# Block-sparse attention with a gated MLP on one core: gMLP products of batch 0 dealt one a slot, and the last spatial product in two halves with a transposition moved to ScalarE

## The chip, the cores and the metric

The kernel runs on one core of a Trainium2 chip. The metric is the device time of one execution in microseconds (us); lower is better. Short names: PE is TensorE, PEld its weight loads, DVE is VectorE, ACT is ScalarE, POOL is GpSimd, SP is SyncE. SP and ACT can also issue DMAs; SPq and ACTq are their DMA issues in the profile.

## The reference

Attention with a block mask over 4 batches, 8 heads, 768 positions and 64 dimensions a head, and a gated MLP with a spatial product (gMLP) on its output:

```
scores = q @ k.T / sqrt(64), masked outside band, edge and sampled blocks
x      = softmax(scores) @ v, heads side by side          # (4, 768, 512)
h      = relu(x @ w_in);  u, v = two halves of h          # 512 columns each
v_n    = (v - mean) / sqrt(var + 1e-6)                    # over the columns
v_s    = w_spatial @ v_n + b_spatial                      # over the 768 positions
out    = (u * v_s) @ w_out                                # float32
```

## The kernel before, in words

The 768 positions are six chunks of 128 (`tcc` 0 to 5 in the code). Work is in bfloat16 with float32 sums in PSUM.

**Slots.** The order of all instructions is written out by hand (`manual_schedule`). The main loop (L882) runs over slots. From slot 36 on, a slot does one sixth of one head: `qk_full` issues two score matmuls (L487) into a PSUM tile `ps` and one exponential on ACT (L491) that reads it; `av_full` issues six matmuls with the values (L538) for the head seven slots behind. The tile `ps` has the tag `sc`, of which there are two buffers: the score matmuls of slot s can start only when the exponential of slot s-2 has read its tile. Behind these, `run_queue(STEPS.get(s))` (L896) takes a number of gMLP matmul steps from a queue. For slots 20 to 97 that number stands in the dictionary `STEPS` (L816); from slot 98 on it is dealt evenly.

**The gMLP of a batch** (class `Moe`) is a list of products. Each is made by `product` (L610): some matmuls of 512 columns into one PSUM tile (all at L617), the last followed by `done`, which takes the result out. `v_product` and `u_product` make v and u. `s_product` is the spatial product of one chunk: six matmuls, and then one DVE instruction (L689) that adds the bias and multiplies by u, in place in the tile `un`. Behind every second chunk it issues a DMA transposition from `un` into `gt` (L699) on SP. `o_product` is the product with `w_out`: four matmuls that read `gt` as weights, an eviction to `osb` by ACT or DVE, and the DMA of the output (L718).

**The last batch** (`self.last`) has its spatial and output products behind the loop (L901), where PE has nothing else to do. There the transposition of chunks 0 and 1 and that of chunks 2 and 3 are each one DMA, and chunks 4 and 5 have one each: G01, G23, G4 and G5 below. The spatial products are called s0 to s5 and the output products o0 to o5; o5 is already in two halves of 256 columns, o5a and o5b. ACT evicts o0, o2, o4 and o5b, DVE o1, o3 and o5a. ACT issues the output DMAs of o0, o1, o2 and o5b, SP those of o3, o4 and o5a. Every engine runs its instructions in their order, and an instruction that waits holds up all behind it. PSUM tiles of the tail go round three tags (`tail_tags`, L594), six banks in all.

Of the kernel before, what the change touches and what calls it, by code (L numbers as in the profile page):

```python
# [14 lines left out]
ALU = mybir.AluOpType  # L15
# [11 lines left out]
def kernel(  # L27
# [16 lines left out]
    nc = tc.nc  # L44
# [5 lines left out]
    NCH = S // 128  # L50
# [3 lines left out]
    DH = DFF // 2  # L54
# [24 lines left out]
    w_spt = const.tile([128, NCH, NCH, 128], BF16)  # L79
    b_col = const.tile([128, NCH], FP32)  # L80
# [517 lines left out]
    def moe_ps(last):  # L598
        if not (last or ended):
            return psum.tile([128, 512], FP32, tag=moe_tag(), bufs=1, name="ps_moe")  # L600
        if not last:
            return psum.tile([128, 1024], FP32, tag="sc", bufs=2, name="ps_sc")[:, 0:512]
        tail_tags.rotate(1)
        if tail_tags[0] == "sc":
            return psum.tile([128, 1024], FP32, tag="sc", bufs=2, name="ps_sc")[:, 0:512]
        if tail_tags[0] == "moe":
            return psum.tile([128, 512], FP32, tag=moe_tag(), bufs=1, name="ps_t")
        return psum.tile([128, 512], FP32, tag="av", bufs=2, name="ps_t")

    def product(n, lhs, rhs, last, done, w=512):  # L610
        ref = {}
        out = []
        for i in range(n):
            def run(i=i):
                if i == 0:
                    ref["ps"] = moe_ps(last)
                nc.tensor.matmul(out=ref["ps"][:, 0:w], lhsT=lhs(i), rhs=rhs(i),  # L617
                                 start=(i == 0), stop=(i == n - 1))
                if i == n - 1:
                    done(ref["ps"][:, 0:w])  # L620
            out.append(run)
        return out
# [6 lines left out]
    class Moe:  # L629
# [55 lines left out]
                           self.last, done)  # L685

        def s_product(self, tcc):
            def done(ps):
                nc.vector.scalar_tensor_tensor(out=self.un[:, tcc, :], in0=ps,  # L689
                                               scalar=b_col[:, tcc:tcc + 1],  # L690
                                               in1=self.un[:, tcc, :], op0=ALU.add,
                                               op1=ALU.mult)
                if self.last and tcc >= NCH - 2:
                    g0 = tcc
                elif tcc % 2 == 1:
                    g0 = tcc - 1
                else:
                    return
                nc.sync.dma_start_transpose(  # L699
                    out=self.gt[:, g0:tcc + 1].rearrange("p t c n -> p (t c) n"),  # L700
                    in_=self.un[:, g0:tcc + 1, :].rearrange("p t d -> p (t d)"))
            return product(NCH, lambda s: w_spt[:, tcc, s, :], lambda s: self.vn[:, s, :],
                           self.last, done)

        def o_product(self, tcc):
            steps = []
# [37 lines left out]
    def deal(steps, slots):  # L744
        queue.extend(steps)
        pace["slots"], pace["credit"] = slots, 0.0

    def run_queue(n=None):
        if n is not None:
            for _ in range(n):  # L750
                queue.popleft()()
            return
        if not queue or pace["slots"] <= 0:
            return
        pace["credit"] += (len(queue) - pace["credit"]) / pace["slots"]
        pace["slots"] -= 1
        n = int(pace["credit"] + 0.5)
        for _ in range(min(n, len(queue))):
            queue.popleft()()
            pace["credit"] -= 1  # L760
# [5 lines left out]
    def when(slot, *fns):  # L766
        at.setdefault(slot, []).extend(fns)
# [45 lines left out]
    when(18, lambda: first["steps"].popleft()())  # L813
    when(20, close_first)
    when(29, lambda: deal(moe[0].in_steps("v2 v3 u2 u3", TC), 14))
    STEPS = {20: 0, 21: 3, 22: 2, 23: 0, 24: 2, 25: 1, 26: 2, 27: 2, 28: 0, 29: 1, 30: 1, 31: 1, 32: 2, 33: 1, 34: 1, 35: 1, 36: 1, 37: 0, 38: 1, 39: 2, 40: 2, 41: 2, 42: 1, 43: 3, 44: 3, 45: 0, 46: 2, 47: 1, 48: 2, 49: 1, 50: 2, 51: 0, 52: 2, 53: 1, 54: 1, 55: 1, 56: 1, 57: 2, 58: 1, 59: 1, 60: 1, 61: 2, 62: 2, 63: 1, 64: 1, 65: 1, 66: 1, 67: 2, 68: 2, 69: 1, 70: 1, 71: 1, 72: 1, 73: 1, 74: 2, 75: 1, 76: 1, 77: 2, 78: 1, 79: 1, 80: 1, 81: 1, 82: 0, 83: 2, 84: 1, 85: 2, 86: 0, 87: 1, 88: 1, 89: 2, 90: 2, 91: 0, 92: 2, 93: 2, 94: 2, 95: 2, 96: 2, 97: 2}  # L816
    when(42, lambda: deal(moe[0].in_steps("v4 v5 u4 u5", TC) + moe[0].rest_steps(),
                          S0 + 8 + 48 - 42))
    for b in (1, 2):
# [62 lines left out]
    for s in range(NS + LAG + 2):  # L882
# [11 lines left out]
        for f in early:  # L894
            f()
        run_queue(STEPS.get(s))  # L896
        for f in late.get(s, []):
# [34 lines left out]
```

## Time and profile before

| what | us |
|---|---|
| median of 3 runs | 209.09 (209.01 to 209.22) |
| the profiled execution, its own time | 209.45 |
| its span, first to last instruction | 207.6 |
| PE busy | 202.7 |
| ACT busy | 167.0 |
| DVE busy | 129.9 |

The profile is of one execution. Times in it run from the start of the span. The granted clock of PE is 1.00 in it. A line of a timeline gives start, length, engine, line of the code, operation, tiles and number of instructions; instructions of one kind that follow each other are merged, and a bracket at the end is idle time of the engine before it and what ended that. A DMA landing is the time from issue until its semaphore is complete.

### The profile page before, as it was taken

To read this page: it belongs to the slowest core of one execution; us is meant where nothing else is said; L and a number is where in the kernel's file an instruction comes from. 1 tells how busy PE (TensorE), PEld (TensorE's weight loads), DVE (VectorE), ACT (ScalarE), POOL (GpSimd) and SP (SyncE) were. 2 spreads that over 40 slices of the span, in tenths; PEclk is the share of its full clock that TensorE was granted. 3 is DMA by queue.
4 is the path that set the end of the run, shared out by engine and by line. 5 is a ranking of instruction groups with operands and counts; after the bars stand their busy time and mean duration, and the time that the engine had idled before them with its cause. 6 is when DMAs were issued, how large, how long until landed. Compare 5 with 4: busy or idle time off the path is not lost.

```text
span 207.6 us, 5255 instructions
## 1 busy us (share of the span) xinstructions
PE 202.7 (98%) x2128; PEld 127.2 (61%) x2128; DVE 129.9 (63%) x287; ACT 167.0 (80%) x222; POOL 75.4 (36%) x117
## 2 busy tenths in 40 slices
PE   8899999999999999999999999999999999999993
PEld 6689878766666666655655555655665556444441
DVE  7688697889654364648798355348685444567542
ACT  5899999999999999889999887998989883266022
POOL 6799899684680421310716402200202000003000
PEclk9999999999999999999999999999999999999999
DMA  5999999999999999999986549785101072810466
GB/s 141 345 364 347 345 406 297 234 278 303 230 356 193 264 272 171 319 318 262 299 91 182 162 88 279 179 246 125 38 3 38 0 92 51 285 72 0 50 152 255
DMA packets 65579, 42.21 MB, mean 203 GB/s; under 512 B 46740, under 2 KB 60436, under 8 KB 65556
## 3 DMA queue, kind: packets, MB, share of 16 engines
q1 hardware_dynamic: 64692, 40.78, 76.8%
q10 hardware_dynamic: 864, 1.11, 1.5%
q8 instruction: 16, 0.26, 0.5%
q14 instruction: 7, 0.06, 0.1%
HBM read 24.38 MB, written 6.29 MB: 148 GB/s over the span
## 4 chain that ended last, share of the span: by engine, by line
PE 93%; ACT 5%; issue 0%; DVE 0%; ACTq 0%
PE ps_moe L617 32%; PE ps L487 23%; PE ps_av L538 13%; PE ps_t L617 8%; PE ps L474 6%; PE ps_sc L617 5%; ACT a_all L479 5%; PE ps_av L520 4%; PE wps L182 1%; PE ps L302 1%; PE ps_av L302 1%; PE mq L309 0%; ACT osb L224 0%; PE psq L317 0%; PE ps L317 0%
## 5 line engine op out<-in xcount | busy, mean ns | idle before, releaser
L491 ACT ACTIVATE a_all<-ps 128x768 bf16<-128x768 f32 x144 | 112.8, 812 | 11.8 <-PE ps L487 5.3
L487 PE MATMUL ps<-kq 88*128 88x384 bf16 x288 | 70.4, 325 | 0.0
L538 PEld LDWEIGHTS <-a_all 128*128 128x128 bf16 x864 | 45.2, 97 | 20.0
L538 PE MATMUL ps_av<-vv,a_all 128*128 128x65 bf16 x864 | 49.8, 193 | 0.0
L487 PEld LDWEIGHTS <-kq 88*128 88x128 bf16 x288 | 27.7, 97 | 29.2 <-issue 0.3
L617 PE MATMUL ps_moe<-w_in_t,xt 128*128 128x512 bf16 x144 | 43.2, 378 | 0.0
L479 ACT ACTIVATE a_all<-ps 128x1024 bf16<-128x1024 f32 x36 | 34.1, 1026 | 2.5 <-PE ps L474 2.0
L617 PE MATMUL ps_moe<-vn,w_spt 128*128 128x512 bf16 x108 | 33.5, 378 | 0.0
L656 POOL TENSOR_SCALAR std<-mv 128x3 f32<-128x3 f32 (+1 forms) x9 | 2.9, 317 | 72.5 <-DVE mv L653 56.9
L138 POOL CAST nat<-st_k 128x768 bf16<-128x768 f32 (+2 forms) x18 | 14.6, 810 | 30.8 <-DMA st_k<-in_k_dram 29.9
L502 DVE RECIPROCAL rc<-ps_av 128x6 f32<-128x6 f32 (+1 forms) x36 | 6.7, 186 | 26.0 <-PE ps_av L538 23.2
L689 DVE SCALAR_TENSOR_TENSOR un<-ps_moe,b_col,un 128x512 bf16<-128x512 f32 x18 | 13.5, 749 | 14.8 <-PE ps_moe L617 14.8
L474 PE MATMUL ps<-kq 88*128 88x256 bf16 (+3 forms) x140 | 22.0, 279 | 0.7 <-ACT a_all L479 0.3
L617 PEld LDWEIGHTS <-xt 128*128 128x128 bf16 x192 | 15.4, 98 | 7.5 <-DVE xt L221 0.2
L503 DVE TENSOR_TENSOR xn<-ps_av,rc 128x384 bf16<-128x384 f32 (+1 forms) x36 | 18.5, 513 | 1.2
L617 PE MATMUL ps_moe<-w_out_t,gt 128*128 128x512 bf16 x60 | 17.6, 378 | 0.0
L652 DVE BATCH_NORM_STATS2 stats<-vn 128x6 f32<-128x512 bf16 x24 | 16.4, 683 | 1.3 <-ACT vn L647 0.9
L474 PEld LDWEIGHTS <-kq 88*128 88x128 bf16 (+1 forms) x140 | 12.8, 98 | 5.2 <-DVE kq L221 0.8
L138 POOL CAST nat<-st_q 128x768 bf16<-128x768 f32 (+2 forms) x21 | 14.8, 706 | 2.7 <-DMA st_q<-in_q_dram 2.2
L188 DVE TENSOR_SCALAR vn<-ps_moe 128x512 bf16<-128x512 f32 x18 | 12.3, 686 | 4.6 <-PE ps_moe L617 4.5
L617 PEld LDWEIGHTS <-w_spt 128*128 128x128 bf16 x144 | 11.7, 98 | 5.2
L221 DVE COPY kq<-tt 64x1536 bf16<-64x1536 bf16 x24 | 14.4, 598 | 0.4
(85 smaller groups left out, 208.7 us busy)
## 6 DMA issues: line engine op xcount, KB each, us to landing
st_v<-in_v_dram SPq DMA_DIRECT2D x16, 384.0 KB, 5.8
st_k<-in_k_dram SPq DMA_DIRECT2D x15, 384.0 KB, 4.7
out_dram<-osb SPq DMA_DIRECT2D x20, 256.0 KB, 2.8
st_q<-in_q_dram SPq DMA_DIRECT2D x12, 384.0 KB, 4.5
w_f<-in_moe_w_in_dram SPq DMA_DIRECT2D x6, 256.0 KB, 6.6
ws_f<-in_moe_w_spatial_dram SPq DMA_DIRECT2D x4, 384.0 KB, 7.2
w_f<-in_moe_w_out_dram SPq DMA_DIRECT2D x4, 256.0 KB, 4.2
st_q<-in_q_dram SPq DMA_DIRECT2D x6, 128.0 KB, 5.6
```

What stands on the lines that cost most here:

```text
L138: eng.tensor_copy(out=dst, in_=src)
L188: nc.vector.tensor_scalar(out=out, in0=in0, scalar1=s1, scalar2=s2, op0=o0, **kw)
L221: nc.vector.tensor_copy(out=o, in_=i)
L474: nc.tensor.matmul(out=ps[:, at:at + n * TW], lhsT=kq[0:kr, h, ci * 128:(ci + 1) * 128], rhs=kq[0:kr, h, qcols(t0, n)], start=True, stop=True)
L479: nc.scalar.activation(out=out, in_=ps, func=AF.Exp, scale=0.125)
L487: nc.tensor.matmul(out=ps[:, hf * 512:hf * 512 + HALF], lhsT=kq[0:KR, j % H, ci * 128:(ci + 1) * 128], rhs=kq[0:KR, j % H, S + hf * HALF:S ...
L491: nc.scalar.activation(out=a_ref["h", j][:, ci, :].rearrange("p (b c) -> p b c", b=2), in_=ps.rearrange("p (b c) -> p b c", b=2)[:, :, 0:H ...
L503: nc.vector.tensor_tensor(out=out, in0=ps[:, :, 0:D], in1=rc[:, 0:n].to_broadcast([128, n, D]), op=ALU.mult)
L538: nc.tensor.matmul(out=av_ref[j][:, qc, 0:VA], lhsT=a_ref["h", j][:, ci, qc * 128:(qc + 1) * 128], rhs=vv[p % NVV][:, h, ci, 0:VA], start= ...
L617: nc.tensor.matmul(out=ref["ps"][:, 0:w], lhsT=lhs(i), rhs=rhs(i), start=(i == 0), stop=(i == n - 1))
L652: nc.vector.bn_stats(out=stats, in_=self.vn[:, tcc, :])
L689: nc.vector.scalar_tensor_tensor(out=self.un[:, tcc, :], in0=ps, scalar=b_col[:, tcc:tcc + 1], in1=self.un[:, tcc, :], op0=ALU.add, op1=AL ...
```

## The change

The entries of `STEPS` for slots 82 to 91 go from 0, 2, 1, 2, 0, 1, 1, 2, 2, 0 to 1, 1, 1, 1, 1, 1, 1, 2, 1, 1; both sum to 11. In the last batch, the spatial product of chunk 5 is made as two products of 256 columns, each with its own PSUM tile, its own six matmuls and its own DVE instruction; G5 comes behind the second. G4 is issued by ACT; G01, G23 and G5 stay on SP.

```diff
         def s_product(self, tcc):
-            def done(ps):
...
+            parts = 2 if self.last and tcc == NCH - 1 else 1
+            w = DH // parts
+            steps = []
+            for i in range(parts):
+                cs = slice(i * w, (i + 1) * w)
+
+                def done(ps, i=i, cs=cs):
+                    nc.vector.scalar_tensor_tensor(out=self.un[:, tcc, cs], in0=ps,
+                                                   scalar=b_col[:, tcc:tcc + 1],
+                                                   in1=self.un[:, tcc, cs], op0=ALU.add,
+                                                   op1=ALU.mult)
+                    if i < parts - 1:
+                        return
...
-                nc.sync.dma_start_transpose(
+                    (nc.scalar if self.last and tcc == NCH - 2 else nc.sync).dma_start_transpose(
                         out=self.gt[:, g0:tcc + 1].rearrange("p t c n -> p (t c) n"),
                         in_=self.un[:, g0:tcc + 1, :].rearrange("p t d -> p (t d)"))
-            return product(NCH, lambda s: w_spt[:, tcc, s, :], lambda s: self.vn[:, s, :],
-                           self.last, done)
+                steps += product(NCH, lambda s: w_spt[:, tcc, s, :],
+                                 lambda s, cs=cs: self.vn[:, s, cs], self.last, done, w)
+            return steps
...
     STEPS = {
...
-        82: 0, 83: 2, 84: 1, 85: 2, 86: 0, 87: 1, 88: 1, 89: 2, 90: 2, 91: 0,
+        82: 1, 83: 1, 84: 1, 85: 1, 86: 1, 87: 1, 88: 1, 89: 2, 90: 1, 91: 1,
...
```

More of the change, by code (lines that the diff above doesn't have):

```diff
@@ L687, in s_product @@
         def s_product(self, tcc):
-            def done(ps):
[L689 to L701, printed above, removed]
-            return product(NCH, lambda s: w_spt[:, tcc, s, :], lambda s: self.vn[:, s, :],
-                           self.last, done)
+            parts = 2 if self.last and tcc == NCH - 1 else 1
[10 more added lines that the diff above has]
+                        return
+                    if self.last and tcc >= NCH - 2:
+                        g0 = tcc
+                    elif tcc % 2 == 1:
+                        g0 = tcc - 1
+                    else:
+                        return
+                    (nc.scalar if self.last and tcc == NCH - 2 else nc.sync).dma_start_transpose(
+                        out=self.gt[:, g0:tcc + 1].rearrange("p t c n -> p (t c) n"),
+                        in_=self.un[:, g0:tcc + 1, :].rearrange("p t d -> p (t d)"))
+                steps += product(NCH, lambda s: w_spt[:, tcc, s, :],
+                                 lambda s, cs=cs: self.vn[:, s, cs], self.last, done, w)
+            return steps
         def o_product(self, tcc):
@@ L815 @@
     when(29, lambda: deal(moe[0].in_steps("v2 v3 u2 u3", TC), 14))
-    STEPS = {20: 0, 21: 3, 22: 2, 23: 0, 24: 2, 25: 1, 26: 2, 27: 2, 28: 0, 29: 1, 30: 1, 31: 1, 32: 2, 33: 1, 34: 1, 35: 1, 36: 1, 37: 0, 38: 1, 39: 2, 40: 2, 41: 2, 42: 1, 43: 3, 44: 3, 45: 0, 46: 2, 47: 1, 48: 2, 49: 1, 50: 2, 51: 0, 52: 2, 53: 1, 54: 1, 55: 1, 56: 1, 57: 2, 58: 1, 59: 1, 60: 1, 61: 2, 62: 2, 63: 1, 64: 1, 65: 1, 66: 1, 67: 2, 68: 2, 69: 1, 70: 1, 71: 1, 72: 1, 73: 1, 74: 2, 75: 1, 76: 1, 77: 2, 78: 1, 79: 1, 80: 1, 81: 1, 82: 0, 83: 2, 84: 1, 85: 2, 86: 0, 87: 1, 88: 1, 89: 2, 90: 2, 91: 0, 92: 2, 93: 2, 94: 2, 95: 2, 96: 2, 97: 2}
+    STEPS = {20: 0, 21: 3, 22: 2, 23: 0, 24: 2, 25: 1, 26: 2, 27: 2, 28: 0, 29: 1, 30: 1, 31: 1, 32: 2, 33: 1, 34: 1, 35: 1, 36: 1, 37: 0, 38: 1, 39: 2, 40: 2, 41: 2, 42: 1, 43: 3, 44: 3, 45: 0, 46: 2, 47: 1, 48: 2, 49: 1, 50: 2, 51: 0, 52: 2, 53: 1, 54: 1, 55: 1, 56: 1, 57: 2, 58: 1, 59: 1, 60: 1, 61: 2, 62: 2, 63: 1, 64: 1, 65: 1, 66: 1, 67: 2, 68: 2, 69: 1, 70: 1, 71: 1, 72: 1, 73: 1, 74: 2, 75: 1, 76: 1, 77: 2, 78: 1, 79: 1, 80: 1, 81: 1, 82: 1, 83: 1, 84: 1, 85: 1, 86: 1, 87: 1, 88: 1, 89: 2, 90: 1, 91: 1, 92: 2, 93: 2, 94: 2, 95: 2, 96: 2, 97: 2}
     when(42, lambda: deal(moe[0].in_steps("v4 v5 u4 u5", TC) + moe[0].rest_steps(),
```

## The prediction

> **What bounds the kernel now.** I read the page's busy times and the chain that ended last first.
>
> ```profile
> PE 202.7 (98%) x2128; PEld 127.2 (61%) x2128; DVE 129.9 (63%) x287; ACT 167.0 (80%) x222; POOL 75.4 (36%) x117
> PE 93%; ACT 5%; issue 0%; DVE 0%; ACTq 0%
> ```
>
> PE is busy nearly throughout and the chain runs along it. So a microsecond that PE stands still is a microsecond of the total, and one saved comes out at the end as long as nothing else ends later there. "Busy" hides short stalls, because the ends of matmuls are modelled; stalls are read from starts. Next, therefore, PE's timeline around slot 82 (the score matmuls at 77.08 are the 47th pair), with ACT's for the same stretch and the stretch as one row.
>
> ```profile
> 77.08 0.49 PE L487 MATMUL ps<-kq 88*128 88x384 bf16 x2
> 77.41 0.35 PE L538 MATMUL ps_av<-vv,a_all 128*128 128x65 bf16 x6
> 77.75 0.48 PE L487 MATMUL ps<-kq 88*128 88x384 bf16 x2
> ...
> 78.68 0.49 PE L487 MATMUL ps<-kq 88*128 88x384 bf16 x2
> ...
> 79.41 0.49 PE L487 MATMUL ps<-kq 88*128 88x384 bf16 x2
> ...
> 80.35 0.49 PE L487 MATMUL ps<-kq 88*128 88x384 bf16 x2
> ...
> 80.86 0.49 PE L487 MATMUL ps<-kq 88*128 88x384 bf16 x2
> ...
> 81.74 0.48 PE L487 MATMUL ps<-kq 88*128 88x384 bf16 x2
> ```
>
> ```profile
> 76.16 2.96 ACT L491 ACTIVATE a_all<-ps 128x768 bf16<-128x768 f32 x4
> ```
>
> ```profile
> L491 ACT ACTIVATE a_all<-ps 128x768 bf16<-128x768 f32 x144 | 112.8, 812 | 11.8 <-PE ps L487 5.3
> ```
>
> ```profile
> 77.08:84.86 7.78, 7.78 (x93) 4.90 (x91) 4.50 (x10) 7.28 (x10) 1.66 (x2) 1.00 1.26 238
> ```
>
> Start to start, slot 84 with one gMLP step takes 79.41 - 78.68 = 0.73, slot 85 with two takes 0.94, slot 86 with none 0.51. But slot 82, also with none, takes 77.75 - 77.08 = 0.67, and slot 87 with one takes 0.88. Both are about 0.15 too long. Four exponentials take 2.96, each 0.81 long (the page's group, 812 ns), so one starts every (2.96 - 0.81)/3 = 0.72. The second of them, slot 81's, ends near 76.16 + 0.72 + 0.81 = 77.69, and slot 83's scores start at 77.75: they wait for its PSUM tile. A slot without a gMLP step is shorter than an exponential, so two slots later PE waits for ACT.
>
> Then the tail, in the timeline of SP and PE's weight loads, with each transposition's time to landing.
>
> ```profile
> 198.66 1.22 SPq L699 DMA_TRANSPOSE gt<-un  x1
> ```
>
> ```profile
> 199.98 1.22 SPq L699 DMA_TRANSPOSE gt<-un  x1
> ```
>
> ```profile
> 197.34 3.86 SPq L699 DMA_TRANSPOSE gt<-un  x3
> ...
> 197.85 0.75 DVE L689 SCALAR_TENSOR_TENSOR un<-ps_t,b_col,un 128x512 bf16<-128x512 f32 x1 [0.55 <-PE ps_t L617]
> ...
> 199.15 0.75 DVE L689 SCALAR_TENSOR_TENSOR un<-ps_sc,b_col,un 128x512 bf16<-128x512 f32 x1 [0.54 <-PE ps_sc L617]
> ...
> 200.56 0.15 PEld L617 LDWEIGHTS <-gt 128*128 128x128 bf16 x2 [0.28 <-DMA gt<-un]
> ```
>
> ```profile
> gt<-un SPq DMA_TRANSPOSE x1, 3.2
> ```
>
> ```profile
> gt<-un SPq DMA_TRANSPOSE x1, 2.5
> ```
>
> ```profile
> 203.31 0.77 PEld L617 LDWEIGHTS <-gt 128*128 128x128 bf16 x8 [0.45 <-DMA gt<-un]
> ```
>
> G23 is issued at 197.34 and lands 3.2 later (first landing row); its reader o2 loads weights at 200.56. G4 is issued at 198.66 and lands after 2.5 (second row). G5 is issued at 199.98 and o5 loads from it at 203.31, so it takes 3.3. The three are in flight together on SP's queue, each issued as the one before it has left SP.
>
> **Part 1: the slots.** The work is the same eleven steps. Without stalls before: three slots of 0.51, three of 0.73 and four of 0.94 make 7.48; the row shows 7.78, so 0.30 is stall. After: nine slots of 0.73 and one of 0.94 make 7.51, so about 0.27 to 0.30 goes; I take 0.29, the two stalls of 0.15. No new wait comes: at 0.73 a slot PE stays behind the 0.72 of the exponentials. Chunk 2's output product ends one slot later than before, three slots ahead of the next use of its bank, and in the built order one output DMA on SP moves behind a transposition whose reader is seven slots off. PE is the bound from there to the tail, so 0.29 arrives. Bounds: 0 (something later absorbs it) and 0.30.
>
> **Part 2: halves.** PE's and DVE's timelines at the end show both widths:
>
> ```profile
> 202.55 0.81 PE L617 MATMUL ps_t<-w_out_t,gt 128*128 128x512 bf16 x3
> 203.31 0.61 PE L617 MATMUL ps_sc<-w_out_t,gt 128*128 128x256 bf16 x4
> 203.76 0.60 PE L617 MATMUL ps_t<-w_out_t,gt 128*128 128x256 bf16 x4
> ```
>
> ```profile
> 202.53 0.69 DVE L221 COPY osb<-ps_t 128x512 f32<-128x512 f32 x1 [1.03 <-PE ps_t L617]
> 203.96 0.42 DVE L221 COPY osb<-ps_sc 128x256 f32<-128x256 f32 x1 [0.74 <-PE ps_sc L617]
> ```
>
> Six matmuls of 512 columns become twelve of 256. Four of 256 take 203.76 - 203.31 = 0.45, so 0.11 each and 1.33 for twelve. The last three of o4 take 0.81 with 0.38 for one alone, so 0.216 a step and 1.30 for six: +0.03. The last DVE piece shrinks from 0.75 to about 0.48 (estimate: the copies go from 0.69 to 0.42 between 512 and 256 columns), so chunk 5 is ready 0.26 earlier, at 199.65. That would be a gain for G5 if G5 could start then.
>
> **Part 2: G4 on ACT.** This is the term that decides. The changed kernel's instructions, with the semaphores each waits for, stand so on ACT and on SP:
>
> ```
> ACT L707 DmaTransposeAnt gt<-un 128x4x128 [waits DMAHW3,DMAHW5,DMAHW2,DMAHW6,DMAHW1,DMAHW7,DMAHW0,DVE]
> ACT L224 Activation osb<-ps_t 128x512 [waits PE,Activation]
> SP  L707 DmaTransposeAnt gt<-un 128x4x128 [waits DMAHW0,DMAHW1,DVE,Activation]
> SP  L727 DMACopy out_dram<-osb 128x512 [waits DMAHW5,DVE]
> ```
>
> Each DMA counts up one of eight semaphores, DMAHW0 to 7, when it has landed. Of DMAHW7, G4 asks the count that G23's landing makes; of DMAHW0, G5 asks the count that G4's landing makes. Before, G4 and G5 ask only for their data and an old DMA. So transpositions that were in flight together now go one at a time: G23 lands, then G4 is issued, lands, then G5 is issued. [...]
>
> Worked on the old clock, part 1 left aside: G23 has landed at 200.55. G4 issues on ACT at 200.60 (0.05 to pass the wait: landing at 197.34 + 3.2, reader at 200.56). It lands 2.5 later at 203.10; nothing else moves then, as with G4 before. G5 issues at 203.20 and lands, by its own 3.3, at 206.50. Its lower bound is G4's 2.5; its upper one the longest landing of an L699:
>
> ```profile
> L699 SPq DMA_TRANSPOSE gt<-un x13: 1217/1232/2532, 62.5 to 200.0; - x13
> ...
> DMA to landing us min/median/max: 2.5/3.2/4.8
> ```
>
> I take 3.3, since like G5 before it runs beside output DMAs. ACT's timeline has what is queued behind G4 there:
>
> ```profile
> 199.99 0.60 ACT L224 ACTIVATE osb<-ps_t 128x512 f32<-128x512 f32 x1 [8.09 <-PE ps_t L617]
> ```
>
> On ACT, G4 stands ahead of that eviction of o0, which starts at 199.99 before and at about 201.87 now (200.60 and 1.22 of issue), and with it all of o0 to o2's output; PE does not wait for those banks, as only o5b reuses one. On SP, G5 stands ahead of the outputs of o3, o4 and o5a. PE reaches o4 at 202.33 (one step ahead of 202.55) and waits until 203.15, then stands from about 204.0 until 206.5. From o5's weight load to the end of the span the old tail takes 207.6 - 203.31 = 4.3:
>
> ```profile
> 203.25 1.60 SPq L718 DMA_DIRECT2D out_dram<-osb  x3
> ...
> 204.86 0.34 ACTq L718 DMA_DIRECT2D out_dram<-osb  x1
> ```
>
> ```profile
> GB/s 396 370 423 212 265 291 396 264 423 344 396 423 396 317 304 330 383 344 317 370 291 370 357 225 66 0 0 0 0 0 0 0 0 0 0 0 0 0 0 0
> ```
>
> That last row is the DMA traffic from 204.5 to 207.6: without a pause until 206.5, so o5's two outputs of 128 KB queued behind o4's. In the new tail o0 to o4 are out before o5 starts, which takes 0.2 off (estimate; between 0 and the 0.35 that 128 KB takes at 370 GB/s). So the span would end at 206.5 + 4.3 - 0.2 = 210.6, which is +3.0.
>
> **Sum.** +3.0 - 0.29 = +2.7; the 0.03 of the halves lies on PE ahead of a wait and costs nothing. Span 207.6 to 210.3, the profiled execution 209.45 to 212.15. That execution is 0.36 above the median of the runs, so against the median: 209.09 + 2.7 = **211.8**. G5's landing bounds make 211.0 (2.5) to 213.3 (4.8).
>
> **The rivals.**
>
> *The waits cost nothing (208.8).* G4 issues as soon as DVE's 197.85 + 0.75 is done, at 198.66, and G5 at 199.72 without waiting for it. The point that decides is whether ACT's transposition starts ahead of 200.5. Then G5 lands ahead of 203.2, and o5 no longer waits its 0.12 (o4's last matmul starts at 202.55 + 2 x 0.216 = 202.98 and could be followed at 203.20; o5 starts at 203.31). But the row of traffic shows the outputs of o4 to o5b back to back, so an earlier o5 queues longer, and that gain is at most 0.1. This gives 209.09 - 0.29 - (0 to 0.1) = 208.7 to 208.8. For it speaks that no transposition of the trace shows such a wait; against it, the list of waits. 6%, two thirds of it within 0.2%.
>
> *Only the first wait costs (210.5).* G4 waits for G23, but G5 starts at 199.7 since the count it asks for is reached early. Then o4 reads at 203.15, and the last outputs hang on ACT's queue, late by 201.87 - 199.99 = 1.9, which the steady traffic hands on nearly whole: 209.09 + 1.7 - 0.29 = 210.5. Against it stands DMAHW0 in G5's list. 9%.
>
> *G5 lands late and PE's clock falls (213.4 to 214.3).* If G5 takes 4.8 beside the outputs, PE stands idle for 3.8 and o5's eight matmuls (203.31 to 204.36) might run at half clock: 213.3 and up to 0.9 more. The trace shows a granted clock of 1.00 throughout and no such gap. [...] 10%.
>
> **How the numbers follow.** Forecast 75%, rivals 6, 9 and 10%. The range 210.4 to 213.2 takes in nearly all of the forecast's bounds and the second rival, and leaves out the first rival and most of the third. 0.2% (0.42 us) is about what a measurement of this kernel can tell from no change. Faster by more than that: 2%, the lower end of the first rival with luck; within: 4%; slower: 94%.
>
> **What would show it.** Right: ACT's transposition issues just after o2's weight load; SP's last one issues some 2.6 later; PE has two gaps, near 0.8 ahead of o4 and near 2.5 ahead of o5; ACT evicts o0 1.9 late; slots 82 to 88 go by 0.73 each without a stall. Wrong: an ACT transposition that overlaps G23's flight; a G5 issued ahead of G4's landing; ACT needing far more than 1.22 to issue one; or stalls in slots 82 to 91 that only move.

## The result and the profile after

The changed kernel takes 211.72 us (median of 4 runs, 211.39 to 211.93); the kernel before 209.14 (209.01 to 209.22). The ratio is 1.0107 with a 95% interval of 1.0081 to 1.0134: slower by 2.6 us, where 2.7 was forecast. The profiled execution took 211.93 with a span of 210.1.

The page's busy times and its chain that ended last:

```profile
PE 202.6 (96%) x2134; PEld 127.5 (61%) x2134; DVE 130.1 (62%) x288; ACT 167.0 (79%) x222; POOL 74.8 (36%) x117
PE 92%; ACT 4%; DMA 1%; DVE 0%; issue 0%; ACTq 0%
```

PE does nearly the same work in a longer span, and DMA has come into the chain. The end of that chain in order of time:

```profile
201.92 0.53 DVE osb L221
202.45 3.05 DMA gt<-un
205.50 0.05 issue
205.54 1.54 PE ps_t L617 x8
207.08 0.03 ACTq L224
207.11 0.05 issue
207.16 0.38 ACT osb L224
```

For 3.05 the end hangs on G5 alone. PE's, ACT's and SP's timelines, and the landing row of ACT's transposition, show what stands before it:

```profile
202.35 1.04 PE L617 MATMUL ps_sc<-w_out_t,gt 128*128 128x512 bf16 x4 [0.47 <-DMA gt<-un]
205.54 1.52 PE L617 MATMUL ps_t<-w_out_t,gt 128*128 128x256 bf16 x8 [2.16 <-DMA gt<-un]
```

```profile
199.84 1.27 ACTq L707 DMA_TRANSPOSE gt<-un  x1
201.21 0.60 ACT L224 ACTIVATE osb<-ps_t 128x512 f32<-128x512 f32 x1 [9.93 <-PE ps_t L617]
```

```profile
196.71 1.23 SPq L707 DMA_TRANSPOSE gt<-un  x1
```

```profile
202.45 1.21 SPq L707 DMA_TRANSPOSE gt<-un  x1
```

```profile
gt<-un ACTq DMA_TRANSPOSE x1, 2.5
```

G23 is issued at 196.71 and G4 3.13 later, where it was 1.33 later before; its data had been there since 197.98 (DVE's 197.23 + 0.75). G4 lands after 2.5, and then G5 is issued. PE stands 0.47 ahead of o4 and 2.16 ahead of o5. DVE's rows show that the halves did their part: chunk 5 was ready at 198.95, 3.5 ahead of G5's issue.

```profile
197.23 0.75 DVE L695 SCALAR_TENSOR_TENSOR un<-ps_t,b_col,un 128x512 bf16<-128x512 f32 x1 [0.54 <-PE ps_t L617]
197.89 0.48 DVE L695 SCALAR_TENSOR_TENSOR un<-ps_sc,b_col,un 128x256 bf16<-128x256 f32 x1
198.47 0.48 DVE L695 SCALAR_TENSOR_TENSOR un<-ps_t,b_col,un 128x256 bf16<-128x256 f32 x1
```

A view by stretches (length, busy time by engine, then PE's granted clock, DMA share and GB/s) has slots 82 to 91 and the time around o5:

```profile
76.73:84.21 7.48, 7.48 (x92) 4.83 (x91) 4.56 (x9) 7.29 (x11) 1.66 (x2) 1.00 1.23 219
203.40:205.54 2.14, 0.00 (x0) 0.00 (x0) 0.00 (x0) 0.60 (x1) 0.00 (x0) 1.00 1.06 324
205.54:205.97 0.43, 0.42 (x4) 0.40 (x5) 0.00 (x0) 0.00 (x0) 0.00 (x0) 1.00 1.02 400
205.97:207.10 1.13, 1.10 (x6) 0.47 (x4) 0.42 (x1) 0.00 (x0) 0.00 (x0) 0.50 0.75 292
```

The ten slots take 7.48 where they took 7.78. In the middle of o5 PE's granted clock falls from 1.00 to 0.50 in this execution.

### The profile page after: what moved, and what is told of

Its sections match the earlier page's. It is cut to its first block, busy times and chain, and to the rows that moved or that the text cites. A ratio compares the mean times of both kernels' runs of the same rounds, so it can differ in the third digit from the quotient of the medians.

```text
span 210.1 us, 5270 instructions
## 1 busy us (share of the span) xinstructions
PE 202.6 (96%) x2134; PEld 127.5 (61%) x2134; DVE 130.1 (62%) x288; ACT 167.0 (79%) x222; POOL 74.8 (36%) x117
## 3 DMA queue, kind: packets, MB, share of 16 engines
q10 hardware_dynamic: 1408, 1.25, 1.9%
## 4 chain that ended last, share of the span: by engine, by line
PE 92%; ACT 4%; DMA 1%; DVE 0%; issue 0%; ACTq 0%
PE ps_moe L617 32%; PE ps L487 22%; PE ps_av L538 13%; PE ps_t L617 8%; PE ps L474 6%; PE ps_sc L617 4%; ACT a_all L479 4%; PE ps_av L520 3%; DMA gt<-un 1%; PE wps L182 1%; PE ps L302 1%; PE ps_av L302 1%; ACT kq L224 0%; DVE osb L221 0%; PE ps L317 0%
## 5 line engine op out<-in xcount | busy, mean ns | idle before, releaser
L138 POOL CAST nat<-st_k 128x768 bf16<-128x768 f32 (+2 forms) x18 | 13.9, 774 | 32.0 <-DMA st_k<-in_k_dram 30.9
L617 PE MATMUL ps_moe<-w_out_t,gt 128*128 128x512 bf16 x60 | 18.1, 378 | 0.0
L474 PEld LDWEIGHTS <-kq 88*128 88x128 bf16 (+1 forms) x140 | 12.7, 97 | 5.3 <-DVE kq L221 1.0
L617 PEld LDWEIGHTS <-w_spt 128*128 128x128 bf16 x150 | 12.3, 98 | 4.8
L221 DVE COPY kq<-tt 64x1536 bf16<-64x1536 bf16 x24 | 15.0, 625 | 0.4
(85 smaller groups left out, 208.9 us busy)
```

The lines of the kernel that those rows point to most:

```text
L138: eng.tensor_copy(out=dst, in_=src)
L221: nc.vector.tensor_copy(out=o, in_=i)
L474: nc.tensor.matmul(out=ps[:, at:at + n * TW], lhsT=kq[0:kr, h, ci * 128:(ci + 1) * 128], rhs=kq[0:kr, h, qcols(t0, n)], start=True, stop=True)
```

## The experiments

The theory: by the waits in the changed kernel's list, G23, G4 and G5 run in series. The main rival: a transposition on ACT holds up what is queued behind it there, the evictions and outputs of o0, o2 and o4. Two smaller ones: the halves or the slots cost something.

Medians scatter by more than some of these effects, because the first part of the kernel, which no edit touches, does: slot 82 begins anywhere between 76.4 and 77.4 in the fourteen profiles. So beside the medians stand two distances from the profiles: from G23's issue to o5's first matmul, and from G23's issue to the end of the span. From slot 92 to G23's issue it is 112.5 in every one.

| kernel | median us | ratio to before, 95% interval | slots 82 to 91 | G23 to o5 | G23 to end |
|---|---|---|---|---|---|
| before | 209.1 to 209.3 | | 7.77 | 5.97 | 10.3 |
| changed | 211.72 | 1.0081 to 1.0134 | 7.48 | 8.83 | 13.4 |
| e1_slots | 208.91 | 0.9975 to 0.9998 | 7.48 | 5.98 | 10.3 |
| e2_halves | 209.31 | 0.9997 to 1.0014 | 7.77 | 5.98 | 10.3 |
| e3_act | 212.36 | 1.0128 to 1.0170 | 7.77 | 8.93 | 13.9 |
| e4_slots_halves | 209.02 | 0.9978 to 1.0008 | 7.48 | 5.97 | 10.3 |
| e5_all_act | 209.82 | 1.0008 to 1.0043 | 7.48 | 5.91 | 11.1 |
| e6_g4_g5_act | 211.47 | 1.0074 to 1.0124 | 7.48 | 6.98 | 12.7 |
| e7_g5_act | 211.13 | 1.0058 to 1.0109 | 7.48 | 6.50 | 12.4 |
| e8_filler | 213.18 | 1.0155 to 1.0206 | 7.48 | 10.49 | 14.7 |
| e9_filler_wide | 212.03 | 1.0115 to 1.0175 | 7.48 | 8.84 | 13.1 |
| e10_act_free | 211.80 | 1.0105 to 1.0144 | 7.48 | 8.92 | 13.2 |
| e11_all_act_free | 209.16 | 0.9986 to 1.0014 | 7.48 | 6.02 | 10.5 |
| e12_g5_act_free | 210.54 | 1.0039 to 1.0072 | 7.48 | 7.26 | 11.8 |

**The parts of the change, one by one.** `e1_slots` is the kernel before with the new step counts:

```diff
-        82: 0, 83: 2, 84: 1, 85: 2, 86: 0, 87: 1, 88: 1, 89: 2, 90: 2, 91: 0,
+        82: 1, 83: 1, 84: 1, 85: 1, 86: 1, 87: 1, 88: 1, 89: 2, 90: 1, 91: 1,
```

> Only the new step counts for slots 82 to 91; the tail as before. Theory (two stalls of 0.15 us go and PE carries the gain to the end): 208.8 to 208.9 us beside 209.1 before, slots 82 to 88 at 0.73 each. Rival (the gain is absorbed later): 209.1.

It measured 208.91 beside 209.25 for the kernel before on the same chip, 0.34 less; the row of its stretch agrees with the theory to a hundredth.

```profile
76.46:83.95 7.49, 7.44 (x92) 4.83 (x92) 4.00 (x9) 7.30 (x11) 2.49 (x3) 1.00 1.16 270
```

`e2_halves` has the halves, with all transpositions on SP and the old step counts (first edit, against the changed kernel; the step counts are not shown); `e3_act` has G4 on ACT and nothing else (second edit, against the kernel before):

```diff
-            (nc.scalar if self.last and tcc == NCH - 2 else nc.sync).dma_start_transpose(
+            nc.sync.dma_start_transpose(
```

```diff
-                nc.sync.dma_start_transpose(
+                (nc.scalar if self.last and tcc == NCH - 2 else nc.sync).dma_start_transpose(
```

> Only the last spatial product in two halves; all transpositions on SP, step counts as before. Theory (o5 starts up to 0.12 earlier, but its outputs queue behind o4's): 209.0 to 209.15, the last transposition issued about 0.26 earlier. Rival (the earlier transposition counts in full): 208.9. Rival (the halves are what made the changed kernel slow): above 210.

> Only the transposition of chunk 4 on ScalarE; the last spatial product whole, step counts as before. Theory (transpositions of two queues go one at a time, so G23, G4 and G5 run in series): 211.9 to 212.1, that is the changed kernel's time and the 0.29 of the slots. Rival (it takes the halves as well): clearly below 211.5.

`e2_halves` takes 209.31 beside 209.25 for the kernel before on the same chip, the same within the interval. Next to no change was expected (209.0 to 209.15), but for another reason: o5 starts no earlier, 5.98 behind G23, and G5 is issued 2.65 behind it as before. SP's row holds three issues without a gap, so SP is busy with G4 until then, and data that are ready earlier help nothing.

```profile
197.20 3.86 SPq L707 DMA_TRANSPOSE gt<-un  x3
```

`e3_act` alone makes the whole loss: 212.36, somewhat above what was expected. Its PE, and its granted clock ahead of o5 and through it:

```profile
202.90 1.04 PE L617 MATMUL ps_t<-w_out_t,gt 128*128 128x512 bf16 x4 [0.50 <-DMA gt<-un]
206.18 1.04 PE L617 MATMUL ps_sc<-w_out_t,gt 128*128 128x256 bf16 x4 [2.24 <-DMA gt<-un]
207.01 1.06 PE L617 MATMUL ps_t<-w_out_t,gt 128*128 128x256 bf16 x4
```

```profile
205.64:206.18 0.54, 0.00 (x0) 0.00 (x1) 0.00 (x0) 0.00 (x0) 0.00 (x0) 0.50 1.06 406
206.18:208.10 1.92, 1.89 (x8) 1.04 (x8) 0.42 (x1) 0.00 (x0) 0.00 (x0) 0.50 0.67 256
```

The gaps are those of the changed kernel, so the halves have no share in the loss. Here the clock had fallen ahead of o5, and both its halves run slow: o5b starts 0.83 behind o5a, where the kernel before has 0.45. That is most of what the profile is over the changed kernel's.

`e4_slots_halves` is the changed kernel with the one word back, `nc.sync` for G4.

> The changed kernel with the transposition of chunk 4 back on SP. Theory: 208.7 to 208.9, below both kernels; all of the loss goes with the one word. Rival (halves or slots cost something too): 209.1 or more.

It takes 209.02, a little above the 208.7 to 208.9 expected (the kernel before takes 209.25 on that chip), with a tail of 10.3 as before. All of the loss goes with that word. Its interval reaches over 1, so it is not shown to beat the kernel before; `e1_slots` is, by 0.02 to 0.25%, and has the lowest median here.

**Waits between queues, or ScalarE's queue?** `e5_all_act` puts all four transpositions of the last batch on ACT, `e6_g4_g5_act` G4 and G5, `e7_g5_act` G5 alone; the changed kernel is the base:

```diff
-(nc.scalar if self.last and tcc == NCH - 2 else nc.sync).dma_start_transpose(
+(nc.scalar if self.last else nc.sync).dma_start_transpose(                        # e5
+(nc.scalar if self.last and tcc >= NCH - 2 else nc.sync).dma_start_transpose(     # e6
+(nc.scalar if self.last and tcc == NCH - 1 else nc.sync).dma_start_transpose(     # e7
```

> The changed kernel with all four transpositions of the last batch on ScalarE: one queue again, so none waits for another queue's landing, but ScalarE issues four of them ahead of the eviction of o0. Theory (the waits between two queues are the cost): 209.1 to 209.6; what is left is o0's eviction about 1.0 later, handed on as some 0.5. Rival (a transposition issued by ScalarE, and what queues behind it there, is the cost): at least the changed kernel's 211.7.

> The changed kernel with G4 and G5 both on ScalarE: the wait of G4 for G23 stays, that of G5 for G4's landing goes. Theory: G5 issues right behind G4 and o5 starts some 1.5 earlier than in the changed kernel; 209.8 to 210.5. Rival (work behind transpositions on ScalarE is the cost): above 211.7, since ScalarE is held 1.25 longer.

> The changed kernel with G4 on SP and only G5 on ScalarE: one wait between queues, behind G4's landing. Theory: G5 issues some 0.9 later than its data are ready, and o0's eviction waits behind it; 209.5 to 210.2. Rival (one wait costs as much as two, since the last transposition decides alone): 211.5 or more.

`e5_all_act` has the most work queued behind transpositions on ACT, and no wait between queues among the last four: o5 starts 5.91 behind G23, as before, and the time is 209.82. That takes the changed kernel's 211.72 apart: the waits are the larger cost, but ACT's queue costs something too, 0.8 against `e4_slots_halves` and a little over what was expected. ACT's timeline of `e5_all_act`:

```profile
197.01 3.91 ACTq L707 DMA_TRANSPOSE gt<-un  x3
200.97 0.60 ACT L224 ACTIVATE osb<-ps_t 128x512 f32<-128x512 f32 x1 [9.39 <-DMA gt<-un]
```

`e6_g4_g5_act` and `e7_g5_act` missed: 211.47 and 211.13 where 210.5 and 210.2 were the most expected. The part on the wait came out: with one wait instead of two, o5 starts 1.85 and 2.33 earlier than in the changed kernel. But the end comes only 0.7 and 1.0 earlier. In both ACT evicts late. ACT and SP of `e6_g4_g5_act`:

```profile
199.73 2.58 ACTq L707 DMA_TRANSPOSE gt<-un  x2
202.35 0.60 ACT L224 ACTIVATE osb<-ps_t 128x512 f32<-128x512 f32 x1 [11.20 <-DMA gt<-un]
...
204.92 0.60 ACT L224 ACTIVATE osb<-ps_sc 128x512 f32<-128x512 f32 x1 [0.41 <-PE ps_t L617]
```

```profile
205.54 0.85 SPq L727 DMA_DIRECT2D out_dram<-osb  x2
```

PE is done with o5 at 203.56 + 1.05 = 204.61. ACT evicts o0 only at 202.35, and so o4 only at 204.92; the outputs of o4 and o5a leave at 205.54. ACT's backlog has become the bound. So the rival holds as the second in line. In the changed kernel's profile it cost nothing, as ACT stands idle for 2.81 ahead of o5b's eviction (207.16) until PE is done; it decides as soon as one wait goes.

**Without ScalarE's backlog.** `e10_act_free`, `e11_all_act_free` and `e12_g5_act_free` are e6, e5 and e7 with everything but o5b evicted by DVE and issued by SP:

```diff
-                    on_act = (tcc + i) % 2 == 0 if self.last else tcc in O_ACT[self.b]
+                    on_act = i == 1 if self.last else tcc in O_ACT[self.b]
...
-                    (nc.scalar if i or (self.last and tcc < 3) else nc.sync).dma_start(
+                    (nc.scalar if i else nc.sync).dma_start(
```

> G4 and G5 on ScalarE as in the run before, but o0 to o4 and o5a are evicted by DVE and their outputs issued by SP, so that nothing but o5b stands behind the transpositions on ScalarE. Theory (in that run ScalarE's backlog had taken the place of the wait): 209.6 to 210.1. Rival (the one wait left, G4 for G23, costs all of it): 211.4 as before.

> All four transpositions on ScalarE as in the run before, with the evictions of o0 to o4 and o5a on DVE and their outputs on SP. No wait between queues, no backlog. Theory (a transposition issued by ScalarE costs nothing by itself): 208.8 to 209.2. Rival (it is slower from there): 209.8 as before.

> Only G5 on ScalarE as in the run before, with the evictions of o0 to o4 and o5a on DVE and their outputs on SP. One wait between queues, G5 for G4's landing. Theory: 209.1 to 209.6, o5 starting some 0.7 behind o4's end. Rival (one wait costs as much as before, without ScalarE's backlog): 211.1.

`e11_all_act_free`, with no wait and no backlog, is the kernel before again (209.16). A transposition issued by ACT costs by itself nothing that shows: `e4_slots_halves`, where SP issues them all, has 209.02, with runs from 208.6 to 210.6. `e12_g5_act_free`, with one wait, takes 210.54: below the 211.13 with the backlog, but above the 209.6 that was the most expected. `e10_act_free` missed altogether: 211.80, where 210.1 was the most expected. The landing row of ACT's two transpositions (3.2 is G4's; none is on record for G5), G5's issue, and PE:

```profile
gt<-un ACTq DMA_TRANSPOSE x2, 3.2
```

```profile
201.36 1.33 ACTq L707 DMA_TRANSPOSE gt<-un  x1
```

```profile
203.21 1.04 PE L617 MATMUL ps_sc<-w_out_t,gt 128*128 128x512 bf16 x4 [1.21 <-DMA gt<-un]
205.75 1.05 PE L617 MATMUL ps_t<-w_out_t,gt 128*128 128x256 bf16 x8 [1.50 <-DMA gt<-un]
```

G4 takes 3.2 here (the changed kernel: 2.5), and G5 is read 4.4 after its issue (the changed kernel: 205.54 - 202.45 = 3.1). With ACT free, SP issues the outputs of o0 to o3 from 200.16 on, so they are in flight beside G4 and G5. What the backlog had cost comes back as longer flights. Two pairs point the same way: G5 is read 2.5 after its issue in `e6_g4_g5_act` (201.10 to 203.56) and in `e7_g5_act` (200.95 to 203.48), where the first output is issued at 202.51 and 202.89, but 4.4 and 3.3 after it in `e10_act_free` and `e12_g5_act_free` (200.74 to 204.04), where it is issued at 200.16 and 200.12. That the outputs are what slows it is read from such flights, and was not measured by itself.

**PE's clock.** `e8_filler` and `e9_filler_wide` are the changed kernel with matmuls between o4 and o5 that nobody reads, 34 of 128 columns and 9 of 512:

```diff
...
+        if i == len(tail) - 2 * NDH:
+            filler(34, moe_ps(True))                                       # e8
+            to = moe_ps(True)                                              # e9
+            for _ in range(9):
+                nc.tensor.matmul(out=to, lhsT=warm, rhs=w_out_t[:, 0, :], start=True, stop=True)
```

> The changed kernel with 34 matmuls of 128 columns, whose result nobody reads, on PE between o4 and o5, so that PE does not stand still there. The granted clock fell to half in the middle of o5 in the changed kernel's profile. Theory (that fall costs about 0.45): 211.2 to 211.4, o5's matmuls at 0.11 each throughout. Rival (the fall costs nothing, as the end hangs on the outputs): 211.7.

> The changed kernel with 9 matmuls of 512 columns, whose result nobody reads, on PE between o4 and o5 (the run with 34 narrow ones was slowed by something else: G5 took 4.7 to land beside a transfer of 16 KB of instructions). Theory (PE's clock falls in the gap and that costs about 0.45): 211.1 to 211.4, o5's matmuls at 0.11 each, G5 landing after about 3.1 again. Rival (any instructions added on PE there slow G5): 212.5 or more.

`e8_filler` got slower, 213.18, and does not tell what the fall costs: G5 was read 4.7 after its issue. Its DMA traffic from 203.5 to 207.4 has a hole of some 1.5 (15 of 40 parts of about 0.1, in the row below), and a transfer of instructions beside it, on a queue (q8) that carries nothing in this stretch in the profile of the changed kernel:

```profile
GB/s 294 399 336 504 378 357 336 210 152 113 181 197 249 234 255 126 74 8 24 0 21 0 21 0 21 21 21 21 21 18 18 18 171 347 420 462 441 357 336 421
...
q8 instruction: 1, 0.02, 2.3%
```

`e9_filler_wide` adds 18 instructions instead of 68, and its DMA traffic goes on at 320 and 393 GB/s. The rows of its filler and of o5:

```profile
203.70:205.90 2.20, 2.11 (x10) 0.78 (x8) 0.00 (x0) 0.71 (x2) 0.00 (x0) 1.00 1.06 320
206.02:207.10 1.08, 1.05 (x8) 0.70 (x8) 0.42 (x1) 0.00 (x0) 0.00 (x0) 1.00 1.03 393
```

The clock stays at 1.00, and o5's matmuls take 1.05 where the changed kernel's took 1.52. G5 starts o5 8.84 behind G23, as in the changed kernel, and the end comes 0.3 sooner, at 13.1. The median did not follow: 212.03 with runs from 211.65 to 213.69, above what was expected. The profile's slot 82 began at 77.20, 0.47 later than in the changed kernel's, which hides the gain there. So the fall costs about 0.3 to 0.5 by the profiles, and no total shows it.

For the changed kernel's other runs there is an estimate. If the clock is 1.00 up to the fall and 0.50 from there on, as in its profile, then the mean clocks of its four runs (0.990, 0.996, 0.995 and 0.992, over spans of 210.1, 209.9, 209.8 and 209.5) put the fall some 4.2, 1.7, 2.1 and 3.4 ahead of the end of the span. o5's last matmul ends 3.1 ahead of it in the profile. So in two of the four the fall came behind o5, and these two took 211.72, which is the median: there was little in it for the filler to win.

A version in which G4 leaves from ACT without waiting for G23 was not tried, so its time is not known.

## Why the prediction was right

- **The slots: right.** 7.78 to 7.48, and 0.29 in every profile with the new counts. The two stalls are gone and the rest of the kernel passes the gain on.
- **The halves: right that they are worth nothing.** Chunk 5 was ready 198.95 - 196.71 = 2.24 behind G23's issue, where it was 199.90 - 197.34 = 2.56: 0.32 earlier, with 0.26 worked out. But G5 could not start, in the changed kernel for the wait and in `e2_halves` for SP's own issue of G4.
- **G4 on ACT: right, and its terms nearly so.** G23's flight was 3.0 (3.2 forecast), G4's 2.5 (2.5), G5 was read 3.1 after its issue (3.3). o5 starts 8.83 behind G23; the working gave 206.5 - 197.34 = 9.2 and so was 0.3 too long. The list of waits pointed to the right sum, and the profile shows the order: G4 issued 3.13 behind G23, G5 2.61 behind G4. Why the built program has these waits, no run shows.
- **The tail behind o5: mis-sized the other way.** 4.3 - 0.2 = 4.1 was forecast, and 210.1 - 205.54 = 4.6 measured. The step that failed is that PE's clock would stay at 1.00 through the gap ahead of o5, 2.5 in the forecast. No run shows a length of gap up to which it stays there; it fell to 0.50 behind a gap of 2.16, and `e9_filler_wide`, with the gap filled, has the fall gone and o5's matmuls at 1.05. The 0.2 that was taken off for o4's outputs did not come either: with the fall gone, `e9_filler_wide` takes 210.3 - 206.02 = 4.3 from o5 to the end, as the kernel before. In the profile the two errors, the wait and the tail, nearly cancel: from G23 to the end the kernel got 13.4 - 10.3 = 3.1 longer, with 3.0 forecast. That the sum is so close is in part luck.
- **The rivals.** "The waits cost nothing" fell: ACT's transposition starts 3.13 behind G23. "Only the first wait costs" named the right second bound, ACT's output queue, but put it too low: `e6_g4_g5_act` comes nearest to it and takes 211.47, not 210.5. It is not the rival's own case, as ACT issues G5 there too and is held some 1.25 longer; the size for G5 on SP stays open. The third rival's clock fall came true behind a gap of 2.16, where the rival had 3.8; its late landing did not (3.1, where it had 4.8).
- **Against the median.** The profiled pair differs by 210.1 - 207.6 = 2.5. The changed kernel's profile is 0.35 ahead already at slot 82 (76.73 against 77.08), where nothing was changed; what was changed makes 2.85 in it, the 3.1 of the tail less the 0.29 of the slots.

## What to carry to other kernels

Before a DMA transposition is moved to another engine to save issue time, look at which transpositions it then has to wait for: where each waits for the landing of the one before, as here, flights that overlapped add up (3.0, 2.5 and 3.1 here). Here o5 started 2.9 us later, to save an issue of 1.2. When one wait of a tail is taken away, look for what was late behind it; here, behind ACT's late evictions, an o5 that started 1.85 earlier ended the kernel only 0.7 earlier (`e6_g4_g5_act`), and without them G5 was read 4.4 after its issue instead of 2.5 (`e10_act_free`). An experiment that adds instructions can also bring their transfer into the stretch that it means to measure (0.02 MB in `e8_filler`).

## What the runs showed of the hardware that was not expected

- PE's granted clock fell with PE not idle for long. In the changed kernel it fell at 205.97, after 2.16 of idle time and 0.42 of matmuls; in the 3.42 before the fall PE was busy for 1.26 (first row). In `e3_act` it fell at 205.64, with PE idle since 203.94 and busy for 1.21 in the 3.41 before the fall. In `e10_act_free` a stretch of 3.41 with 2.20 busy, in which PE stood 1.21 ahead of o4, brought no fall (second row). `e9_filler_wide` was busy for 2.11 + 1.05 = 3.16 of the 3.40 from 203.70 to 207.10, and the clock stayed at 1.00. So in these stretches the clock fell where PE had less work, but which of the idle time, the work and the time since the start sets the moment was not shown. In the clock's record in two traces it stands at 1.00 for 201.39 on end: from 4.58 to 205.97 in the changed kernel, and from 6.27 to 207.66 in the kernel before, whose span ends at 207.64. By the estimate from the mean clocks above, the fall came ahead of o5's end in two of the changed kernel's four runs and behind it in the other two.

```profile
202.55:205.97 3.42, 1.26 (x8) 0.59 (x7) 0.06 (x1) 1.19 (x2) 0.00 (x0) 1.00 0.99 325
```

```profile
200.57:203.98 3.41, 2.20 (x11) 0.77 (x9) 1.81 (x3) 0.00 (x0) 0.00 (x0) 1.00 0.89 231
```

- A transposition of 128 x 512 landed after 2.5 with nothing beside it (G4 in the changed kernel) and was read as late as 4.4 after its issue beside output DMAs (G5 in `e10_act_free`).
- While 0.02 MB of instructions were fetched, transposition and outputs nearly stood for 1.5, at 0 to 24 GB/s (`e8_filler`, one profile); whether the fetch is the cause was not shown. `e9_filler_wide` has no such hole.
